# Pooled attention and two MLPs on one core: the second tile of the second MLP prepared earlier, and its accumulating matmuls moved by one place

## The chip, the cores and the metric

The kernel runs on one core of one Trainium2 chip. The metric is the device time of the program in microseconds (us), the median of several runs. Before the change three runs took 1678.56, 1679.4 and 1681.44 us, so the median is 1679.4 us.

## The reference

`q`, `k` and `v` have the shape (8, 8, 576, 64). Keys and values are averaged over groups of 8 positions, and attention runs over the 72 pooled positions. Its output is laid out as x, 4608 tokens by 512, and passes two MLPs, each 512 to 2048 to 512:

```python
h = x @ w_in                        # first MLP
g = where(h >= 1, h, where(h <= -1, 0, (h + 1) ** 2 / 4))
x = g @ w_out
h = x @ w_in2                       # second MLP
out = (h / (1 + exp(-h))) @ w_out2
```

Values are carried as pairs of float16 numbers (high and low part), so that each product takes three matmuls.

## The kernel before

**First MLP (A).** It works on 9 tiles of 512 tokens. A tile has 16 steps; a step is one block of 128 hidden values: 12 matmuls for h (`emit_h`, tile `hps`), the activation on ScalarE (ACT) and VectorE (DVE), a split into two float16 parts, and three steps later (`LAG`) 12 matmuls into the four accumulators `y0` to `y3` (`emit_yA`). After the last step of a tile `evac_yA` scales the four accumulators into `y32`, a room of the pool `big`, which has one buffer only, and stores them to DRAM (`ydram`).

**Second MLP (B).** It works on 18 tiles of 256 tokens. `tile_B` prepares a tile in six pieces: `load` reads `yin` from `ydram` into the room `big`; `look` takes the largest absolute value (DVE), spreads it over the partitions by a small matmul (`all_max`, tile `all`) and works out scales; `sums_` makes four sums of blocks on GpSimd (POOL) within `yin`; three `part` pieces split everything into the float16 pair `xh`, `xl` (pool `xs`, two buffers). `room` in the changed kernel is what gets that pair.

`group_B(t, q, ys)` then works on one half (q) of the hidden values with a seven-product scheme in place of eight: products 0 to 6 are 24 matmuls each (`hb`), in two banks of `ps_h` and two of `ps_a`. DVE adds them up to four blocks of h, ACT takes the activation, POOL forms four more combinations, ACT and DVE split seven operands (`g`). The seven accumulating products of a group (`py`, 12 matmuls each, in the order 0, 3, 4, 6, 5, 1, 2, into the banks `y0` to `y3`, two products to a bank) are handed on as a list `ys`, and are issued one by one within the next group by the calls `y(n)`. After the group of q = 0, when the last seven products of the tile before are in, `evac_yB` reads the four banks out with one ACT and seven DVE operations, and the result is stored.

**Order of the work.** The program text gives priorities; a planner orders each engine's instructions ahead of time by its own estimate of when each is ready, so that an instruction can stand ahead of others that come earlier in the text. At run time each engine takes its instructions strictly in that order. SyncE (SP) issues all transfers.

**Around the change.** In the last tile of A the list `pend` holds the six pieces of `tile_B(0)`, one per step from step m = 3. The first weights of B's second product (`wd`, `w4[0:4]`) are loaded during A, the other four after `wctx.close()`, into the room of A's weights. Line numbers: `load` L865, `look` L868 to L874 with its max L111 and its matmul L107, sums L681, splits L354 and L355, adds L910, accumulating products L973 to L975, `evac_yB` L985 to L998, `evac_yA` L846 to L849.

Of the kernel before, what the change touches and what calls it, by code (L numbers as in the profile page):

```python
# [9 lines left out]
F32 = mybir.dt.float32  # L10
F16 = mybir.dt.float16
I32 = mybir.dt.int32
AF = mybir.ActivationFunctionType
# [20 lines left out]
def tile_pooled_attention_two_mlps(  # L34
# [18 lines left out]
    nc = tc.nc  # L53
# [5 lines left out]
    N = 512  # L59
    NTILE = NT // N  # L60
# [632 lines left out]
    def comb_b(z, b11, b12, b21, b22):  # L693

        minus(z[1], b12, b11)
        minus(z[2], b22, z[1])
        minus(z[3], b22, b12)
        minus(z[0], b21, z[2])
# [140 lines left out]
    def evac_yA(t):  # L839
        r = XT.pop(t)  # L840
        cy = sm.tile([128, KD], F32, tag="cy", name="cy")
        ts(cy, e2, r["ge"], 2.0 ** -29, ALU.mult, ALU.mult)
        y = big.tile([128, KD, N], F32, tag="big", name="y32")
        for d, ps in enumerate(acc_t.pop(t)):
            if d % 2:
                ts(y[:, d], ps, cy[:, d:d + 1])  # L846
            else:
                nc.scalar.activation(out=y[:, d], in_=ps, func=AF.Copy, scale=cy[:, d:d + 1])
            nc.sync.dma_start(out=ydram[t][:, d], in_=y[:, d])  # L849


    TB = 256
# [4 lines left out]
    def tile_B(t):  # L857

        r = XB[t] = small(e=1, s=1, c1=1, ge=1, sg=1)
        held = {}  # L860

        def load():
            y = big.tile([128, 2, KD, TB], F32, tag="big", name="yin")
            held["y"], held["z"] = y[:, 0], y[:, 1].rearrange("p n (c f) -> p n c f", c=2)
            nc.sync.dma_start(out=held["y"], in_=ydram[t // 2][:, :, t % 2 * TB:(t % 2 + 1) * TB])  # L865
            held["b"] = held["y"].rearrange("p (h c) (n f) -> p h n c f", h=2, n=2)

        def look():  # L868
            m = sm.tile([128, 1], F32, tag="m1", name="m1")
            abs_max(m, held["y"])  # L870
            to_scale(r["e"], r["s"], m, FLOOR, 12)
            ts(r["c1"], e3, r["e"], 2.0 ** -24, ALU.mult, ALU.mult)
            ts(r["ge"], e3, r["e"], 2.0 ** -2, ALU.mult, ALU.mult)
            bits(r["sg"], r["ge"], -1.0, 254)  # L874

        def sums_():
            b = held["b"]
            comb_b([held["z"][:, n] for n in range(4)], b[:, 0, 0], b[:, 0, 1], b[:, 1, 0], b[:, 1, 1])
            r["x"] = [x.rearrange("p c n -> p (c n)")[:, 0:7 * 256].rearrange("p (n c f) -> p n c f", n=7, c=2)
                      for x in new_x()]  # L880

        def part(a, b, x):
            hi, lo = (y[:, a:b] if b > a + 1 else y[:, a] for y in r["x"])
            split(hi, lo, x(), r["s"])

        return [load, look, sums_, lambda: part(0, 2, lambda: held["b"][:, :, 0]),
                lambda: part(2, 3, lambda: held["b"][:, 1, 1]), lambda: part(3, 7, lambda: held["z"])]

    def group_B(t, q, ys):

        r = XB[t]
        xh, xl = r["x"]
        pool = (gp, gp2)[q]
        gt = {}

        def product(n, i):
            p, tag = ((ps_h, "h"), (ps_a, "a"))[n // 2 % 2]
            ps = p.tile([128, 4, 128], F32, tag=tag, name="hb")
            for j in range(4):
                w = w3[4 * q + j]  # L900
                for k_ in range(2):
                    three(ps[:, j], w[:, 0, i, k_], w[:, 1, i, k_], xh[:, i, k_], xl[:, i, k_],
                          j == 0 and k_ == 0, j == 3 and k_ == 1)
            return ps

        def new_c():
            return cp.tile([128, 4, 128], F32, tag="c", name="c")

        def add(out, x, y):
            nc.vector.tensor_tensor(out=out, in0=x, in1=y, op=ALU.add)  # L910

        def act(x):
            nc.scalar.activation(out=x, in_=x, func=AF.Silu, scale=r["c1"])  # L913

        def halves_of(i, x):
            to = gt[i] = pool.tile([128, 2, N], F16, tag="g", name="g16")
            split(to[:, 0], to[:, 1], x.rearrange("p j n -> p (j n)"), r["sg"])

        def y(n):
            for _ in range(n):  # L920
                if ys:
                    ys.pop(0)()

        c11, u, v, c22, z1, z2, z3, z4 = (new_c() for _ in range(8))
        nc.scalar.copy(out=u, in_=product(0, 0))
        add(c11, u, product(1, 1))
        act(c11)
        halves_of(0, c11)
        y(1)
        add(u, u, product(2, 5))  # L930
        y(1)
        add(v, u, product(3, 6))
        y(1)
        p5 = product(4, 4)
        add(c22, v, p5)
        act(c22)
        add(u, u, p5)
        halves_of(3, c22)
        y(1)
        c12 = u  # L940
        add(c12, u, product(5, 2))
        act(c12)
        plus(z1, c12, c22)
        minus(z3, c11, c12)
        minus(z2, z1, c11)
        y(1)
        c21 = v
        add(c21, v, product(6, 3))
        act(c21)
        halves_of(4, z1)  # L950
        halves_of(6, z3)
        y(1)
        halves_of(5, z2)
        minus(z4, c21, z2)
        halves_of(1, c21)
        halves_of(2, z4)
        y(1)
        if q == 0:
            r["acc"] = [ps_y.tile([128, 2, 256], F32, tag=f"y{k_}", name=f"y{k_}") for k_ in range(4)]

        def py(i):
            out = r["acc"][i // 2][:, i % 2]
            first = q == 0 and i == next(n for n in ORDER if n // 2 == i // 2)
            last = q == 1 and i == [n for n in ORDER if n // 2 == i // 2][-1]
            gh, gl = gt[i][:, 0], gt[i][:, 1]
            for j in range(4):
                f, w = slice(128 * j, 128 * j + 128), w4[4 * q + j]
                three_r(out, gh[:, f], gl[:, f], w[:, 0, i], w[:, 1, i], first and j == 0, last and j == 3)

        return [lambda i=i: py(i) for i in ORDER]  # L970
# [180 lines left out]
    for s in range(KF, LAST + LAG):  # L1151
        T, m = divmod(s, KF)
        if s < LAST:
            emit_h(s, chunk1, XT[T]["x"])
        z = s - 1
        if KF <= z < LAST:
            pre_A(z, XT[z // KF])
            min_A(z, XT[z // KF])
        if KF + 1 <= z <= LAST:
            late["gl"] = split_g(z - 1, XT[(z - 1) // KF])  # L1160
        if KF <= z < LAST:
            mid_A(z, XT[z // KF])
            post_A(z, XT[z // KF])
        for _ in range(2 if KF < s <= KF + XS else 1):
            if slots_left:
                next_slot()
        if not slots_left and b1 is None:
            att_ctx.close()
            b1 = bctx.enter_context(tc.tile_pool(name="b1", bufs=1, reuse_waits="tile"))
        want = todo_n * (s - KF + 1) // (SPREAD * KF // 4)  # L1170
        while todo and todo_n - len(todo) < want:
            paced(todo.pop(0), "gl")
        if b1 and not w3 and len(todo) <= left3:
            for i in range(PIECES):
                w3.append(b1.tile([128, 2, 7, 2, 128], F16, name=f"wc{i}"))
                nc.sync.dma_start(out=w3[i].rearrange("p a n c f -> p a n (c f)"), in_=d3[:, i])
        if w3 and not w4 and not todo:
            conv_ctx.close()
            b1 = bctx.enter_context(tc.tile_pool(name="b1w", bufs=1, reuse_waits="tile"))
            for i in range(4):  # L1180
                w4.append(b1.tile([128, 2, 7, 256], F16, name=f"wd{i}"))
                nc.sync.dma_start(out=w4[i], in_=d4[:, i])
        if T == NTILE - 1 and m == 3:
            pend.extend(tile_B(0))
        if pend:
            pend.pop(0)()
        z = s - LAG
        if z >= KF:
            emit_yA(z)
            if z % KF == KF - 1:  # L1190
                evac_yA(z // KF)

    wctx.close()
    b2 = bctx.enter_context(tc.tile_pool(name="b2", bufs=1, side="right", reuse_waits="tile"))
    for i in range(4, PIECES):
        w4.append(b2.tile([128, 2, 7, 256], F16, name=f"wd{i}"))
# [3 lines left out]
    ys = []  # L1200
    for t in range(NTB):
        for q in range(2):
            if t + 1 < NTB:
                if q == 0:
                    pend.extend(tile_B(t + 1))
                for _ in range(3):
                    pend.pop(0)()
            ys = group_B(t, q, ys)
            if q == 0 and t:
                evac_yB(t - 1)  # L1210
    for f in ys:
        f()
    evac_yB(NTB - 1)
# [31 lines left out]
```

## Time and profile before

| | |
|---|---|
| median of 3 runs | 1679.4 us |
| the profiled execution | 1683.29 us |
| its span, first to last instruction | 1681.4 us |
| granted TensorE clock, mean | 0.965 of full speed |
| TensorE matmuls (PE) busy | 1561.3 us, 93% |
| VectorE (DVE) busy | 1255.0 us, 75% |
| ScalarE (ACT) busy | 894.9 us, 53% |
| GpSimd (POOL) busy | 534.7 us, 32% |
| TensorE leaves A, enters B | at 972.38 us |

Busy time of PE counts a matmul from its issue to its modelled end, and neighbours overlap; a matmul row's duration (0.22 or 0.27 us) is therefore longer than its share of the engine, which is the distance to the next row's start. A bracket at the end of a row of the timeline gives the idle time of that engine ahead of it, and the instruction that ended it.

### The profile page before, as it was taken

How to read it: one execution, taken by the hardware profiler on the slowest of the kernel's cores; microseconds unless marked ns; L12 is line 12 of the kernel's file. 1: busy time of each engine (PE TensorE's matmuls, PEld its weight loads, DVE VectorE, ACT ScalarE, POOL GpSimd, SP SyncE). 2: the span in 40 equal slices, each digit the busy share in tenths (PEclk: the TensorE clock that was granted, in tenths of full speed). 3: DMA queues.
4: the chain of work that ended last, by engine and by line, in shares of the span. 5: the costliest groups of instructions: out<-in, count | busy, mean ns of one | idle time of the engine just before them, and what ended most of it. 6: DMA issues, size and time to landing. Idle time of an engine off the chain costs nothing.

```text
span 1681.4 us, 34695 instructions
## 1 busy us (share of the span) xinstructions
PE 1561.3 (93%) x14406; PEld 1078.8 (64%) x14406; DVE 1255.0 (75%) x2204; ACT 894.9 (53%) x1420; POOL 534.7 (32%) x479
## 2 busy tenths in 40 slices
PE   6894799898999999999999979999999999999998
PEld 6542344344444444444444459999999999999998
DVE  7798887978889787897656338777766777777765
ACT  3577354666747547576655435455444454444543
POOL 1322402332424303333422023443333343334322
PEclk7897899899999999999999989999999999999999
DMA  9435587655646576353454030000100001000000
GB/s 278 129 99 140 140 218 174 145 129 137 166 118 161 141 218 167 98 131 86 133 220 148 0 138 27 27 27 27 37 30 27 27 27 39 27 27 27 27 14 27
DMA packets 217037, 166.35 MB, mean 99 GB/s; under 512 B 153904, under 2 KB 176432, under 8 KB 216880
## 3 DMA queue, kind: packets, MB, share of 16 engines
q1 hardware_dynamic: 216880, 164.14, 35.1%
q8 instruction: 113, 1.85, 0.5%
q14 instruction: 44, 0.36, 0.1%
HBM read 102.76 MB, written 33.55 MB: 81 GB/s over the span
## 4 chain that ended last, share of the span: by engine, by line
PE 31%; DVE 26%; issue 15%; ACT 10%; DMA 8%; POOL 8%; SPq 1%; DVEq 0%; POOLq 0%; ACTq 0%
DMA yin<-y 4%; PE y L120 4%; PE y L122 4%; PE y L121 4%; POOL c L681 4%; DVE sum L420 4%; DVE g L355 4%; PE hps L122 4%; PE hps L121 4%; PE hps L120 4%; DVE g L791 3%; POOL c L684 2%; DVE xl L355 2%; DVE g L820 2%; ACT g L354 2%
## 5 line engine op out<-in xcount | busy, mean ns | idle before, releaser
L121 PE MATMUL hb<-xl,wc 128*128 128x128 f16 x2016 | 349.7, 219 | 0.0
L120 PE MATMUL hb<-xh,wc 128*128 128x128 f16 x2016 | 349.7, 219 | 0.0
L122 PE MATMUL hb<-xh,wc 128*128 128x128 f16 x2016 | 349.7, 219 | 0.0
L355 DVE SCALAR_TENSOR_TENSOR g<-c,tsg,g 128x512 f16<-128x512 f32 x252 | 226.6, 902 | 87.8 <-ACT g L354 87.8
L973 PE MATMUL y<-wd,g 128*128 128x256 f16 x1008 | 274.7, 273 | 14.4 <-DVE ob L986 13.0
L975 PE MATMUL y<-wd,g 128*128 128x256 f16 x1008 | 274.8, 273 | 1.0 <-DVE g L355 0.9
L974 PE MATMUL y<-wd,g 128*128 128x256 f16 x1008 | 274.7, 273 | 0.0
L913 ACT ACTIVATE c<-c,tc 128x512 f32<-128x512 f32 x144 | 103.0, 717 | 258.8 <-DVE c L910 258.8
L120 PE MATMUL y<-g,wb 128*128 128x512 f16 x544 | 207.7, 388 | 17.3 <-ACT wb L212 15.0
L120 PE MATMUL hps<-xh,wa 128*128 128x512 f16 x576 | 221.0, 384 | 1.3 <-ACT g L780 0.9
L354 ACT ACTIVATE g<-c,tsg 128x512 f16<-128x512 f32 x252 | 177.6, 718 | 83.7 <-POOL c L684 51.3
L121 PE MATMUL hps<-xl,wa 128*128 128x512 f16 x576 | 220.9, 383 | 0.3 <-DVE skv L95 0.3
L122 PE MATMUL hps<-xh,wa 128*128 128x512 f16 x576 | 220.6, 384 | 0.0
L910 DVE TENSOR_TENSOR c<-c,hb 128x512 f32<-128x512 f32 x252 | 167.7, 680 | 70.4 <-PE hb L122 70.1
L121 PE MATMUL y<-g,wb 128*128 128x512 f16 x544 | 211.2, 388 | 5.8 <-DVE g L820 5.8
L122 PE MATMUL y<-g,wb 128*128 128x512 f16 x544 | 210.5, 387 | 4.1 <-POOL wb L213 3.9
L121 PEld LDWEIGHTS <-wc 128*128 128x128 f16 x2016 | 197.7, 98 | 2.6
L120 PEld LDWEIGHTS <-wc 128*128 128x128 f16 x2016 | 197.7, 98 | 2.1
L122 PEld LDWEIGHTS <-wc 128*128 128x128 f16 x2016 | 197.7, 98 | 0.2
L791 DVE SCALAR_TENSOR_TENSOR g<-g,tbr,u 128x512 f32<-128x512 f32 x144 | 127.4, 886 | 59.2 <-ACT u L787 58.0
L681 POOL TENSOR_TENSOR c<-c 128x512 f32<-128x512 f32 x108 | 163.8, 1530 | 2.8
L787 ACT ACTIVATE u<-u,trsg 128x512 f32<-128x512 f32 x144 | 103.3, 719 | 103.8 <-DVE u L93 103.8
(179 smaller groups left out, 2719.7 us busy)
## 6 DMA issues: line engine op xcount, KB each, us to landing
raw<-in_moe_w_out_dram SPq DMA_DIRECT2D x24, 1024.0 KB
raw<-in_moe_w_in_dram SPq DMA_DIRECT2D x18, 1024.0 KB
raw<-in_k_dram SPq DMA_DIRECT2D x32, 288.0 KB
raw<-in_v_dram SPq DMA_DIRECT2D x32, 288.0 KB
y<-y SPq DMA_DIRECT2D x36, 256.0 KB
yin<-y SPq DMA_DIRECT2D x18, 512.0 KB
out_dram<-ob SPq DMA_DIRECT2D x36, 256.0 KB
qt<-in_q_dram SPq DMA_DIRECT2D x32, 256.0 KB
```

The lines of the kernel that those rows point to most:

```text
L120: nc.tensor.matmul(out=acc, lhsT=wh, rhs=xh, start=start, stop=False)
L121: nc.tensor.matmul(out=acc, lhsT=wh, rhs=xl, start=False, stop=False)
L122: nc.tensor.matmul(out=acc, lhsT=wl, rhs=xh, start=False, stop=stop)
L354: a = nc.scalar.activation(out=hi, in_=x, func=AF.Copy, scale=s)
L355: return a, nc.vector.scalar_tensor_tensor(out=lo, in0=x, scalar=s, in1=hi, op0=ALU.mult, op1=ALU.subtract)
L681: nc.gpsimd.tensor_tensor(out=out, in0=a, in1=b, op=ALU.subtract)
L787: nc.scalar.activation(out=u_t[s], in_=u_t[s], func=AF.Square, scale=r["rsg"])
L791: return nc.vector.scalar_tensor_tensor(out=g32_t[s], in0=g32_t[s], scalar=r["br"], in1=u_t.pop(s), op0=ALU.subtract, op1=ALU.max)
L910: nc.vector.tensor_tensor(out=out, in0=x, in1=y, op=ALU.add)
L973: nc.tensor.matmul(out=acc, lhsT=xh, rhs=wh, start=start, stop=False)
L974: nc.tensor.matmul(out=acc, lhsT=xh, rhs=wl, start=False, stop=False)
L975: nc.tensor.matmul(out=acc, lhsT=xl, rhs=wh, start=False, stop=stop)
```

## The change

Four edits. Of `tile_B(1)` the first three pieces (load, look, sums) follow those of tile 0 in the last tile of A; its parts come ahead of the second group. To make room in `big`, the last `y32` goes to four tiles of the pool `up`. The pair `xh`, `xl` is asked for at the first part, not at the sums. In a group of q = 1 the first call `y(1)` becomes `y(0)` and the last `y(2)`, so that six of the seven places take one product later. For later tiles the load is issued at the end of the tile two before, and look and sums ahead of the next group, which is the same place in the text as before.

```diff
@@ evac_yA
-        y = big.tile([128, KD, N], F32, tag="big", name="y32")
+        if t < NTILE - 1:
+            y = big.tile([128, KD, N], F32, tag="big", name="y32")
+            ys = [y[:, d] for d in range(KD)]
+        else:
+            ys = [up.tile([128, N], F32, tag="gu"[d % 2], name="y32") for d in range(KD)]
         for d, ps in enumerate(acc_t.pop(t)):
             if d % 2:
-                ts(y[:, d], ps, cy[:, d:d + 1])
+                ts(ys[d], ps, cy[:, d:d + 1])
             else:
-                nc.scalar.activation(out=y[:, d], in_=ps, func=AF.Copy, scale=cy[:, d:d + 1])
-            nc.sync.dma_start(out=ydram[t][:, d], in_=y[:, d])
+                nc.scalar.activation(out=ys[d], in_=ps, func=AF.Copy, scale=cy[:, d:d + 1])
+            nc.sync.dma_start(out=ydram[t][:, d], in_=ys[d])
@@ tile_B
+
+        def room():
             r["x"] = [x.rearrange("p c n -> p (c n)")[:, 0:7 * 256].rearrange("p (n c f) -> p n c f", n=7, c=2)
                       for x in new_x()]
         def part(a, b, x):
+            if a == 0:
+                room()
@@ group_B
         add(c11, u, product(1, 1))
         act(c11)
         halves_of(0, c11)
-        y(1)
+        y(1 - q)
...
         halves_of(2, z4)
-        y(1)
+        y(1 + q)
@@ the last tile of A
         if T == NTILE - 1 and m == 3:
             pend.extend(tile_B(0))
+            rest = tile_B(1)
+            pend.extend(rest[:3])
+            rest = rest[3:]
@@ B
+    pend = rest
...
     for t in range(NTB):
         for q in range(2):
-            if t + 1 < NTB:
-                if q == 0:
-                    pend.extend(tile_B(t + 1))
-                for _ in range(3):
-                    pend.pop(0)()
+            for _ in range(min(len(pend), 3 if q else 2 if t else 0)):
+                pend.pop(0)()
             ys = group_B(t, q, ys)
             if q == 0 and t:
                 evac_yB(t - 1)
+        if t + 2 < NTB:
+            pend = tile_B(t + 2)
+            pend.pop(0)()
```

## Rows read from the trace of the kernel before

**Rows 1.** The page: busy us of an engine, share of the span, instructions.
```profile
PE 1561.3 (93%) x14406; PEld 1078.8 (64%) x14406; DVE 1255.0 (75%) x2204; ACT 894.9 (53%) x1420; POOL 534.7 (32%) x479
```

**Rows 2.** Windows: stretch, length, busy us (instructions) by engine, granted clock, DMA share, GB/s.
```profile
940.00:960.00 20.00, 20.00 (x94) 9.11 (x93) 7.62 (x12) 7.88 (x12) 0.00 (x0) 1.00 0.00 1
...
972.38:1016.50 44.12, 31.57 (x425) 28.61 (x424) 22.87 (x38) 16.60 (x24) 12.89 (x13) 0.88 0.38 132
...
978.65:989.83 11.18, 0.98 (x9) 0.64 (x8) 1.22 (x1) 0.00 (x0) 1.05 (x2) 0.69 0.77 305
...
989.83:993.20 3.37, 3.37 (x29) 3.31 (x30) 2.16 (x10) 1.64 (x3) 1.76 (x3) 0.50 0.02 5
...
1023.85:1063.36 39.51, 37.87 (x514) 35.71 (x512) 30.64 (x52) 19.84 (x30) 14.74 (x12) 1.00 0.08 29
...
1561.80:1599.30 37.50, 36.99 (x501) 34.96 (x499) 27.34 (x47) 18.22 (x28) 14.39 (x12) 1.00 0.08 30
...
1599.30:1636.40 37.10, 37.10 (x508) 35.20 (x506) 25.49 (x39) 16.50 (x26) 11.56 (x8) 1.00 0.05 16
```

**Rows 3.** Waits of PE, 960 to 1016.6 us: us in total, times, longest.
```profile
PE all L107 <- DVE m L111: 10.2, 1, 10.2
```

**Rows 4.** Waits of PE, 1020 us to the end.
```profile
PE y L973 <- DVE ob L986: 13.0, 17, 1.5
```

**Rows 5.** Timeline of PE at the start of B: start, us, operation, count, [idle before].
```profile
979.36 0.27 PE L975 MATMUL y<-wd,g 128*128 128x256 f16 x1
...
989.83 0.80 PE L107 MATMUL all<-ident,m 128*128 128x128 f32 x2 [10.20 <-DVE m L111]
...
1016.28 0.39 PE L107 MATMUL all<-ident,m 128*128 128x128 f32 x2
1016.50 0.22 PE L120 MATMUL hb<-xh,wc 128*128 128x128 f16 x1
```

**Rows 6.** Timeline of DVE at the start of B.
```profile
977.56 0.75 DVE L355 SCALAR_TENSOR_TENSOR g<-c,tsg,g 128x512 f16<-128x512 f32 x1 [1.54 <-ACT g L354]
988.56 1.22 DVE L111 TENSOR_REDUCE m<-yin 128x1 f32<-128x1024 f32 x1 [10.25 <-DMA yin<-y]
```

**Rows 7.** Timeline of SP's issues around the end of A.
```profile
972.00 1.82 SPq L849 DMA_DIRECT2D y<-y  x4
973.91 2.19 SPq L1197 DMA_DIRECT2D wd<-d  x4
978.64 0.55 SPq L865 DMA_DIRECT2D yin<-y  x1
```

**Rows 8.** Timeline of POOL at the start of B.
```profile
988.78 2.89 POOL L681 TENSOR_TENSOR yin<-yin 128x256 f32<-128x256 f32 x4 [79.45 <-DMA yin<-y]
```

**Rows 9.** The tile yin: duration ns min/median/max, first and last start.
```profile
L354 ACT ACTIVATE xh<-yin,ts x54: 492/722/1137, 912.5 to 1597.0; 128x512 f16<-128x512 f32 x18, 128x256 f16<-128x256 f32 x18, 128x1024 f16<-128x1024 f32 x18
```

**Rows 10.** Timeline of ACT at the end of A.
```profile
971.28 0.69 ACT L848 ACTIVATE y<-y,cy 128x512 f32<-128x512 f32 x1 [5.52 <-PE y L122]
```

**Rows 11.** Timeline of PE in two groups of q = 1, tiles 10 and 8.
```profile
1382.73 0.22 PE L120 MATMUL hb<-xh,wc 128*128 128x128 f16 x1
...
1385.41 0.27 PE L973 MATMUL y<-wd,g 128*128 128x256 f16 x1
...
1388.77 0.27 PE L973 MATMUL y<-wd,g 128*128 128x256 f16 x1 [0.49 <-DVE ob L986]
...
1305.32 0.22 PE L120 MATMUL hb<-xh,wc 128*128 128x128 f16 x1
...
1312.80 0.27 PE L973 MATMUL y<-wd,g 128*128 128x256 f16 x1 [1.49 <-DVE ob L986]
```

**Rows 12.** Timeline of DVE in the first of these groups.
```profile
1383.88 0.48 DVE L986 SCALAR_TENSOR_TENSOR ob<-y,cyb,ub 128x256 f32<-128x256 f32 x1
...
1388.25 0.86 DVE L986 SCALAR_TENSOR_TENSOR ob<-y,cyb,ub 128x256 f32<-128x256 f32 x2
1389.03 0.67 DVE L910 TENSOR_TENSOR c<-c,hb 128x512 f32<-128x512 f32 x1
```

## The prediction, made before the changed kernel ran

> **What bounds the kernel now.** I read the page first: TensorE (PE) is busy 93% of the span [rows 1], so the question is where its 7% go and which of that the change touches. The windows place it. In A the engine is busy in every microsecond (20.00 of 20.00 at clock 1.00), while DVE works 7.62 and POOL nothing [rows 2]: A is bound by PE, and small work put beside it has cover. At the step from A to B PE has 31.57 busy of 44.12 us. In the steady part of B, 15 tiles take from 1023.85 to 1599.30, 575.45 us (the first and the last window of them are shown), 38.36 us each, against 37.10 us for the tile behind them, in which PE is busy without a gap [rows 2]. That tile has no scale matmul `all`; one costs 0.22 us (1016.28 to 1016.50 [rows 5]), so a tile without waits is 37.32 us, and 15 of them lose 575.45 - 15 x 37.32 = 15.65 us. The list of waits names the causes: one wait of 10.2 us for the max of tile 1 [rows 3], and 17 waits of 13.0 us together for `evac_yB` to free a bank [rows 4]. (13.0 is idle alone; the distance between starts adds some 0.17 us each, which gives the 15.65.)
>
> **Part 1: tile 1 prepared within A.** The order of events in the old transition: the last `y32` is stored from `big` and the four `wd` are issued from 973.91; only then, at 978.64, does SP issue `yin` of tile 1, since `big` was taken [rows 7]. DVE, strictly in order, stands before the max of that tile until 988.56 [rows 6], some 9.9 us after the issue; PE stands before its `all` from the end of the last matmul (979.36 + 0.11) to 989.83, 10.36 us [rows 5]. The granted clock then is 0.50 for the 3.37 us after the stall, the lower level of 1.2 GHz [rows 2]; at the upper level these take half, 1.7 us less. The stall and its slow stretch are worth 10.36 + 1.7 = 12.05 us.
>
> What is moved, and its cover. Load, four sums and max go before the end of A, when `big` is free (tile 0's parts are done there, and no `y32` follows in it). POOL stood idle for 79.45 us before these sums, whose 2.89 us [rows 8] therefore push nothing. The max is 1.22 us on DVE [rows 6], with seven tiny operations after it, in A's 38% loaded DVE [rows 2]. The `all` costs PE 0.22 us there as here. On SP the load passes the four stores and the `wd`, 0.55 us of issue ahead of them [rows 7]. So I take 0 for the move; if the cover failed, DVE would stand before a late load in A, at the worst 9.9 us as here; below zero I see nothing, as PE has no gap in A to give back. The parts of tile 1 (three splits on each engine, at most 1.14 us each on ACT [rows 9]) become possible when A's last `hps` matmul has read its pair; ACT has 5.52 us free before it reads the accumulators [rows 10]. The four small rooms for the last y cost nothing: the same four copies, in rooms that the last steps of A have left; the other bound is one copy's delay, 0.69 us [rows 10].
>
> What is late next at the transition: 14 products at 1.34 us (48 matmuls from 1382.73 to 1385.41 are 2.68) and 7 accumulating ones of 1.31 us (37.10 = 14 x (1.34 + 1.31)) make 27.93 us, with the two `all` 28.4, of the 44.12. After 12.05 some 3.7 us of other waits remain, ACT, POOL and DVE coming late with the first g. Some of it may go, since POOL no longer has tile 1's sums in B; I leave all 3.7 in, keeping 0 and 3.7 as bounds of a further gain. Part 1: **12.05 us**.
>
> For tile 2 the trace has a hint on the queue. What was issued at 978.64 behind the four `wd` landed only 9.9 us later [rows 6, 7]. The Trainium skill, "DMA: Bandwidth & Descriptors", section "Queues, rings and completion order", says that each DMA engine consumes descriptors in ring order: by that rule a later load cannot pass the `wd`, and if `yin` of tile 2 is issued behind them it is as late as tile 1's was; the trace agrees. Priced as rival A.
>
> **Part 2: the accumulating products one place later.** In a group of q = 1 the second accumulating product (the first into its bank) waits for DVE's last readings of the old tile: PE at 1388.77, DVE's last pair beginning at 1388.25 [rows 11, 12]. From the group's start at 1382.73 this is 6.04 us. Before it PE has three products and one accumulating one; after the change four and one, 4 x 1.34 + 1.31 = 6.67 us, so the bank is free 0.63 us before it is asked for. The first accumulating product (bank `y0`) also moves 1.34 us back. Where the wait is longest, tile 8, the release is 1312.80 - 1305.32 = 7.48 us after the start [rows 11], and 0.81 us of wait remain. Five tiles have waits of this kind (1.26 to 1.49 us), ten have 0.46 to 0.70 (the rows show one of each). For the five I take a remainder of 2.2 us in all, between 0 and 5 x 0.81 = 4.1. The gain is 15.65 - 2.2 = **13.45 us**.
>
> Behind the moved product stand the rest of PE's queue, and products that wait for DVE's adds. Three products now run in a row; the trace shows two. The third needs a `ps_a` bank, emptied by an add of the group before. I take 0; the other end is one add late, 0.67 us [rows 12], in each of 17 groups, 11.4 us; below zero, the adds can begin 1.31 us earlier. No matmul is added: the two at the group's end are the one taken from its head. In the last tile the seven products that follow PE's last group keep their number, so the tail stays.
>
> The windows show clock 1.00 in all these tiles, short waits included [rows 2]. The Trainium skill, "TensorE: Matmul & The Clock Gate", section "A second HAM failure mode: psum-queue depth-cycling", says that frequent short idles between groups make the clock fall and rise again. By that rule, 15 waits removed would give back 15 slow stretches of 1.7 us as well, 25 us more; the trace disagrees, as 1.00 leaves nothing to give back, and I count none.
>
> **Sum.** 12.05 + 13.45 = 25.5 us. The profiled execution took 1683.29 us, 1.9 around a span of 1681.4; it would become 1657.8. It stands 3.9 us above the median of 1679.4; against the median the forecast is **1653.9 us**.
>
> **The rivals.**
>
> *A, the stall moves to tile 2.* Its load follows tile 1's parts. If the planner sets those after A's end, the load goes out behind the `wd`, and a max set early in DVE's queue stops DVE as before. For: exactly this happened with tile 1 [rows 6, 7]. Against: ACT and DVE have room for the parts before 971.28, so that the load can pass the `wd`, and tile 2's max is needed a whole tile later in the text. DVE would stand from about 980 to 988.6; PE could run some four products (5.4 us) on free banks, and lose 4 to 10 us. With 7 lost: 1661.
>
> *B, the evacuation's wait moves along.* If the planner puts the now earlier adds of products 1 and 2 in front of DVE's last readings, these end 2 x 0.67 = 1.34 us later; the 0.63 us of room turns into 0.71 us of wait, in 15 tiles 10.7, and with the 2.2 part 2 gives 2.8 in place of 13.45: 1664.5. For: DVE shows no idle time from 1383.88 to the add that ends at 1389.70 [rows 12]. Against: the readings come earlier in the text.
>
> *C, tile 1 is not ahead.* The planner keeps its load behind A's end after all, for instance since it sees DVE or `big` as taken; then part 2 alone comes: 1666. Against: the load's room is free a dozen steps earlier.
>
> *D, neither.* A and B at their worst: within 3 us of 1679.4.
>
> *E, slower.* One mechanism: three products in a row, while product 5 reuses the bank that the add of product 1 frees. That add ends at 1389.70 [rows 12]; product 5 would start at 1382.73 + 5 x 1.34 + 3 x 1.31 = 1393.4. It decides from 3.7 us of delay of that add; to eat 25.5 us in 17 groups takes 1.5 us more, 5.2 in all. With DVE 6 us late, 2.3 x 17 = 39 us are lost: 1679.4 - 25.5 + 39 = 1693. For: DVE is the fullest helper, 75%. Against: it has idle stretches in every half tile.
>
> **Chances.** Forecast 0.60; A 0.14; B 0.10; C 0.06; D 0.05; E 0.05. What a measurement of this kernel can tell from no change is about 0.2%, 3.4 us. Faster is the forecast with A, B and C, 0.90; D is the same, 0.05; E is slower, 0.05. The range: at best both losses vanish with the other waits, 12.05 + 3.7 + 15.65 = 31.4, so 1648, less 1.5 for the scatter of the runs (1678.56 to 1681.44): 1646.5. Upward it takes in A, B and C and part 1 alone (1679.4 - 12.05 = 1667.4): 1668.
>
> **What would show it.** Right: PE's wait for the max at the start of B is gone and the clock stays 1.00 there; `yin` of tile 1 is issued in A with PE busy 20.00 of 20 around it; the waits of accumulating products for `evac_yB` fall from 13.0 to about 2 us; 15 tiles take about 562 us. A long DMA wait of DVE just after A's end shows A; the old list of waits shows B; `yin` after 973.91 shows C; waits of product matmuls for adds show E. A gain below 15 us would make the prediction wrong in one of its two parts.

## The result

The changed kernel takes 1650.16 us (median of 4 runs, 1647.97 to 1653.04), the kernel before 1680.35 us in 4 runs (1678.56 to 1681.44): a ratio of 0.9822, 95% interval 0.9801 to 0.9844, or 30.2 us less. The forecast was 1653.9 us, 25.5 less.

### The profile page after: what moved, and what is told of

Read it like the earlier page. It is cut to its first block, busy times and chain, and to the rows that moved or that the text cites. A ratio compares the mean times of both kernels' runs of the same rounds, so it can differ in the third digit from the quotient of the medians.

```text
span 1649.7 us, 34708 instructions
## 1 busy us (share of the span) xinstructions
PE 1558.8 (94%) x14406; PEld 1081.0 (66%) x14406; DVE 1261.8 (76%) x2204; ACT 895.6 (54%) x1420; POOL 533.6 (32%) x479
## 4 chain that ended last, share of the span: by engine, by line
PE 44%; DVE 24%; issue 9%; ACT 9%; DMA 7%; POOL 7%; SPq 0%; DVEq 0%; POOLq 0%; ACTq 0%
DVE sum L420 5%; POOL c L681 4%; PE y L120 4%; PE y L122 3%; PE y L121 3%; PE hps L121 3%; PE hps L120 3%; PE y L981 3%; PE y L983 3%; PE y L982 3%; PE hps L122 3%; PE hb L121 3%; PE hb L120 3%; PE hb L122 3%; DVE g L791 3%
## 5 line engine op out<-in xcount | busy, mean ns | idle before, releaser
L791 DVE SCALAR_TENSOR_TENSOR g<-g,tbr,u 128x512 f32<-128x512 f32 x144 | 123.4, 858 | 56.8 <-ACT u L787 55.6
```

Source lines behind the costliest of these rows:

```text
L791: return nc.vector.scalar_tensor_tensor(out=g32_t[s], in0=g32_t[s], scalar=r["br"], in1=u_t.pop(s), op0=ALU.subtract, op1=ALU.max)
```

## The profile after, beside the one before

Two stages answer for most of it. The first is the transition, from the last accumulating matmul of A to the first product of B's tile 1; the second is all that lies behind. The windows of the changed kernel (columns as in [rows 2]), A's last steps first:

```profile
940.00:966.43 26.43, 26.43 (x124) 11.96 (x122) 11.51 (x17) 11.28 (x17) 0.00 (x0) 1.00 0.06 20
966.43:969.53 3.10, 3.10 (x23) 1.68 (x22) 1.89 (x2) 0.86 (x2) 2.66 (x4) 1.00 0.02 5
969.53:997.18 27.65, 27.65 (x415) 26.70 (x414) 19.18 (x27) 15.95 (x23) 9.57 (x8) 1.00 0.49 173
997.18:1649.70 652.52, 644.22 (x8684) 610.06 (x8681) 478.59 (x797) 314.84 (x477) 241.19 (x198) 1.00 0.08 28
```

A ends at 969.53; nine of B's matmuls (0.50 us) were put ahead of its last twelve, so B's first tile holds TensorE for 27.65 + 0.50 = 28.15 us, where it took 44.12 [rows 2]. The engine is busy in all of it, and the granted clock is 1.00, the upper level, where the kernel before had a stretch at 0.50. That is 15.97 us; 0.22 of it is no gain, since the scale matmul `all` of tile 1 now stands in A. Behind it are 652.5 us where there were 1681.4 - 1016.50 = 664.9: 12.4 us less. The remaining 3.35 us lie ahead, in A and the attention (A's end 972.38 against 969.03). Together 31.7, the difference of the two spans.

SP's issues show the moved load. The first `yin` below is tile 1's, within A; the second is tile 2's, also ahead of the stores and of the four `wd`, where before even tile 1's came behind them [rows 7]:

```profile
913.15 0.54 SPq L869 DMA_DIRECT2D yin<-y  x1
...
963.10 0.52 SPq L869 DMA_DIRECT2D yin<-y  x1
969.21 1.80 SPq L853 DMA_DIRECT2D y<-y  x4
971.09 2.23 SPq L1209 DMA_DIRECT2D wd<-d  x4
```

DVE's two maxima, of tile 1 and tile 2, wait 1.12 and 1.57 us for their transfers where tile 1's waited 10.25 [rows 6]:

```profile
916.76 1.22 DVE L111 TENSOR_REDUCE m<-yin 128x1 f32<-128x1024 f32 x1 [1.12 <-DMA yin<-y]
...
966.68 1.22 DVE L111 TENSOR_REDUCE m<-yin 128x1 f32<-128x1024 f32 x1 [1.57 <-DMA yin<-y]
```

POOL's sums of both tiles lie in A too, where before those of tile 1 ran in B [rows 8]. The third row is POOL's first work in B, a combination of the first group:

```profile
916.87 3.34 POOL L681 TENSOR_TENSOR yin<-yin 128x256 f32<-128x256 f32 x4 [11.06 <-DMA yin<-y]
966.79 2.90 POOL L681 TENSOR_TENSOR yin<-yin 128x256 f32<-128x256 f32 x4 [46.57 <-DMA yin<-y]
978.84 1.27 POOL L684 TENSOR_TENSOR c<-c 128x512 f32<-128x512 f32 x1 [9.15 <-ACT c L921]
```

TensorE's waits from 960 us to the end are one line, where [rows 3] and [rows 4] had 10.2 and 13.0 us:

```profile
PE y L981 <- DVE ob L994: 2.7, 3, 1.4
```

And the steady tiles: tile 1 starts at 997.18, tile 16 at 1560.74, so 15 tiles take 563.6 us (forecast about 562; before, between the same two points, 575.7). The three waits left are in the tiles 7, 8 and 9: 0.54, 0.77 and 1.42 us. The rows of tile 8 and of tile 9, each with the start of its group of q = 1:

```profile
1278.18 0.22 PE L120 MATMUL hb<-xh,wc 128*128 128x128 f16 x1
...
1285.79 0.27 PE L981 MATMUL y<-wd,g 128*128 128x256 f16 x1 [0.77 <-DVE ob L994]
...
1316.44 0.22 PE L120 MATMUL hb<-xh,wc 128*128 128x128 f16 x1
...
1324.70 0.27 PE L981 MATMUL y<-wd,g 128*128 128x256 f16 x1 [1.42 <-DVE ob L994]
```

In tile 8 the bank comes free 7.61 us after the group's start (before, 7.48 [rows 11]). In tile 9 it comes 8.26 us after it, where before it was 6.06. What sets that moment stands further up in DVE's queue: the max of the tile two ahead, which waits for that tile's load. Before, in tiles 8 and 9:

```profile
1299.34 1.22 DVE L111 TENSOR_REDUCE m<-yin 128x1 f32<-128x1024 f32 x1 [3.23 <-DMA yin<-y]
...
1337.34 1.22 DVE L111 TENSOR_REDUCE m<-yin 128x1 f32<-128x1024 f32 x1 [1.80 <-DMA yin<-y]
...
1350.80 0.27 PE L973 MATMUL y<-wd,g 128*128 128x256 f16 x1 [0.51 <-DVE ob L986]
```

And in tile 9 of the changed kernel, SP's issue of the load and DVE's max:

```profile
1305.72 0.53 SPq L869 DMA_DIRECT2D yin<-y  x1
...
1311.23 1.22 DVE L111 TENSOR_REDUCE m<-yin 128x1 f32<-128x1024 f32 x1 [3.73 <-DMA yin<-y]
```

TensorE's waiting matmul starts 13.46 us after the max in tile 8 before (1312.80 [rows 11]), 13.46 in tile 9 before, 13.47 in tile 9 now. In all twelve kernels the readings of that bank end 13.4 us after the max begins in 175 of 180 tiles; the other five are first tiles. So in the steady tiles the waits for the evacuation follow the landing of a load: the max began 5.5 us after the issue in tile 9 now, 3.6 us in tile 9 before. No run moved these loads.

## The experiments

The table gives time and ratio to the kernel before (measured anew with e1 to e4, with e5 to e8, and with e9 and e10: 1680.48, 1679.16 and 1679.04 us). From the profile it gives A's end (without the 0.50 us of products put ahead of it), the transition, what lies behind, and TensorE's waits for the evacuation, all in us. The transitions of 28.4 us (e1, e8) hold two `all`, those of 28.15 one.

| kernel | us | ratio, 95% | A's end | transition | behind | waits for the evacuation |
|---|---|---|---|---|---|---|
| before | 1680.35 | | 972.38 | 44.12 | 664.9 | 13.0 |
| changed | 1650.16 | 0.9801 to 0.9844 | 969.03 | 28.15 | 652.5 | 2.7 |
| e1_rooms | 1661.4 | 0.9876 to 0.9914 | 963.85 | 28.38 | 665.2 | 13.8 |
| e2_shift | 1662.15 | 0.9881 to 0.9912 | 964.75 | 44.86 | 652.8 | 3.0 |
| e3_early | 1663.91 | 0.9885 to 0.9916 | 969.93 | 28.16 | 664.3 | 13.0 |
| e4_wd_after | 1670.42 | 0.9928 to 0.9957 | 965.14 | 36.16 | 663.8 | 12.1 |
| e5_two_places | 1653.62 | 0.9818 to 0.9866 | 968.22 | 28.16 | 654.9 | 1.7 |
| e6_tile2_behind | 1650.5 | 0.9787 to 0.9843 | 961.05 | 28.15 | 650.4 | 1.1 |
| e7_before_again | 1680.86 | 0.9989 to 1.0022 | 970.81 | 44.53 | 665.6 | 13.5 |
| e8_rooms_shift | 1650.13 | 0.9803 to 0.9854 | 966.82 | 28.37 | 653.2 | 3.5 |
| e9_order | 1646.59 | 0.9781 to 0.9825 | 964.62 | 28.15 | 649.5 | 0 |
| e10_after_order | 1649.48 | 0.9799 to 0.9852 | 968.13 | 28.15 | 650.7 | 1.6 |

### e1: the four rooms alone

```diff
-        y = big.tile([128, KD, N], F32, tag="big", name="y32")
+        if t < NTILE - 1:
...
+            ys = [up.tile([128, N], F32, tag="gu"[d % 2], name="y32") for d in range(KD)]
```

> The kernel before with one edit: the last y32 of A leaves through four rooms of the pool up, so that big is free when A ends; the text of tile_B and the accumulating products stay as before. Theory (the stall came from the load of tile 1 being late, because its only room was taken): the planner can now issue that load in A, TensorE's wait for the max at the start of B falls from 10.2 us to under 1, the clock stays 1.00 there, and the time falls by 12 us, 13 to 16 if the other waits of the transition go as well; the evacuation's 17 waits stay at about 13 us. Rival A (the stall moves to tile 2, whose load now goes out behind the wd): a wait of 4 to 10 us appears within 30 us of A's end and the time falls by 2 to 8 us only. Rival C (what counts is the place in the text): no change.

The transition fell by 15.7 us, to no wait at all; the evacuation's waits stayed. The time fell by 19 us, more than the stages behind A give (see e7). With the text of `tile_B` unmoved, SP issued tile 1's load in A all the same, and tile 2's behind the `wd`. First the windows, then SP's issues:

```profile
963.85:992.23 28.38, 28.38 (x426) 27.41 (x425) 23.13 (x38) 17.51 (x26) 12.63 (x11) 1.00 0.54 187
```

```profile
908.26 0.55 SPq L869 DMA_DIRECT2D yin<-y  x1
963.53 1.79 SPq L853 DMA_DIRECT2D y<-y  x4
965.42 2.26 SPq L1201 DMA_DIRECT2D wd<-d  x4
970.42 0.53 SPq L869 DMA_DIRECT2D yin<-y  x1
```

So the room alone was enough to let the load out early. This experiment's rival C (the place in the text) falls. Rival A had its condition, tile 2 behind the `wd`, and its price was zero, by a narrow margin. POOL, which stood for the same load, could start at 981.30, 10.9 us after the issue, so it landed as late as tile 1's did before, or later. DVE had other work until then, and its max followed without idle time:

```profile
981.26 1.21 DVE L111 TENSOR_REDUCE m<-yin 128x1 f32<-128x1024 f32 x1
...
981.30 3.82 POOL L681 TENSOR_TENSOR yin<-yin 128x256 f32<-128x256 f32 x4 [0.50 <-DMA yin<-y]
```

### e2 and e3: each part alone

```diff
 e2, on the kernel before            e3, on the changed kernel
-        y(1)                       -        y(1 - q)
+        y(1 - q)                   +        y(1)
...
-        y(1)                       -        y(1 + q)
+        y(1 + q)                   +        y(1)
```

> The kernel before with one edit: in a group of q = 1 the first y(1) becomes y(0), the last y(2). Theory (the accumulating products came 0.5 to 1.5 us too early for the evacuation, and one product more in front of them covers it): the waits of accumulating products for the evacuation fall from 13.0 to 2 to 4 us, the stall of 10.2 us at the start of B stays, time 12 to 13.5 us less. Rival B (the evacuation's last readings move back as adds come earlier): 10 to 13 us of waits remain, time 0 to 4 us less.

> The changed kernel with y(1) and y(1) put back: only tile 1's earlier preparation and its rooms remain. Theory (the two parts are independent and add up): the transition takes 28.2 us as in the changed kernel, the evacuation's waits are back at 13 us; time 16 us under the kernel before (1664), 12 to 14 above the changed kernel. Rival (the moved accumulating products also fill the first groups of B, so that the last 3.7 us of the transition were theirs): 12 us under the kernel before, with 3 to 4 us of waits of TensorE between A's end and the second tile.

e2: the waits for the evacuation fall to 3.0 us, the stall stays, and what lies behind the transition is 652.8, 12.1 us less. Its whole time fell by 18.3, more than the second MLP gives; its A ended 7.6 us earlier, see e7. TensorE's waits in e2, from A's end on:

```profile
PE all L107 <- DVE m L111: 10.8, 1, 10.8
PE y L973 <- DVE ob L986: 3.0, 4, 1.3
PE y L973 <- ACT g L354: 1.4, 3, 0.7
PE y L975 <- DVE g L355: 0.9, 2, 0.6
```

e3: the transition is 28.16 us as in the changed kernel, with TensorE busy in all of it, and the waits are back at 13.0. In the profiles the two parts add up: from A's end to the end of the span 709.0 before, 697.7 with e2, 692.5 with e3; 11.4 and 16.5 are 27.9, and the changed kernel has 28.3 less. In whole times they do not: 18.3 and 16.6 are 34.9 against 30.2. That the last 3.7 us of the transition belong to the moved products (the rival of e3) is refuted: they are gone without them.

### e4: the queue, without the room

```diff
-        nc.sync.dma_start(out=w4[i], in_=d4[:, i])
...
+            if t == q == 0:
+                with tc.issue_after(late["yin"].ins):
+                    for i in range(4, PIECES):
+                        nc.sync.dma_start(out=w4[i], in_=d4[:, i])
```

> The kernel before with one edit: the four last wd are issued after the load of tile 1 instead of before it; the room big is still taken until A's last y is stored. Theory (most of the 10.2 us is the transfer standing behind 3.6 MB of wd): the load lands 5 to 6 us after its issue or sooner instead of 9.9, TensorE's wait for the max falls to 1 to 4 us, time 7 to 10 us less. Rival (the late room alone is the cause, the queue is not): the wait stays at 8 us or more, time within 2 us of before. If the wd now come too late, waits for DMA appear at the accumulating products of the second group.

The room still comes only after A's end, but the load no longer stands behind the `wd`. It went out at 969.53, 4.4 us after A's end (before, 6.3, with the `wd` issued in between), and DVE had its max at 973.13, 3.6 us later and not 9.9 [rows 6, 7]. TensorE's wait for it is 2.0 us in place of 10.2, of which some 6.3 us come from the shorter way of the load and 1.9 from its earlier issue. The time falls by 10 us, the transition by 8.0. Tile 2's load, behind the `wd` here, was what DVE stood for next:

```profile
973.13 1.22 DVE L111 TENSOR_REDUCE m<-yin 128x1 f32<-128x1024 f32 x1 [2.06 <-DMA yin<-y]
...
986.72 1.22 DVE L111 TENSOR_REDUCE m<-yin 128x1 f32<-128x1024 f32 x1 [3.74 <-DMA yin<-y]
```

```profile
PE y L975 <- DVE g L355: 2.4, 2, 2.2
PE all L107 <- DVE m L111: 2.0, 1, 2.0
PE hb L120 <- DVE c L910: 0.9, 1, 0.9
```

Here rival A is seen at work: DVE idles 3.74 us and TensorE stands 2.2 us behind it for one g. Most of the stall's length was the queue's; that the load was in that queue at all was the room's.

### e5: one more place

```diff
         y(1 - q)
         add(u, u, product(2, 5))
-        y(1)
+        y(1 - q)
...
-        y(1 + q)
+        y(1 + 2 * q)
```

> The changed kernel with the accumulating products of a group of q = 1 one more place later: the first two calls are y(0), the last y(3). Theory (what is left of the waits, 2.7 us at three places, is the same release coming 7 to 8 us after the group's start): they vanish, the part from A's end to the end of the span falls from 680.7 us to 677 to 678, nothing new waits. Rival (without two accumulating products at its head TensorE outruns DVE's adds): waits of product matmuls for adds appear, over 0.2 us in each of 17 groups, and that part grows by 3 us or more.

The theory was wrong: what lies behind the transition grew by 2.4 us. The rival was nearer, but not right either: it asked for 3 us or more and for waits for DVE's adds in each of 17 groups. The old wait didn't go entirely, and a new one came at four places, at products that wait for ACT's copy of the first product out of its bank:

```profile
PE hb L120 <- ACT c L933: 2.6, 4, 1.0
PE y L981 <- DVE ob L994: 1.7, 5, 0.3
```

### e6: tile 2's load held back behind the wd

```diff
-            pend.pop(0)()
+            with tc.issue_after(late["wd"].ins) if t == 0 else nullcontext():
+                pend.pop(0)()
```

> The changed kernel with one edit: the load of tile 2 must be issued behind the four wd. It prices rival A of the prediction. Theory (DVE takes its queue in order and stands before the max of tile 2 until the load lands, as it did for tile 1): the load lands 8 to 11 us after its issue, DVE idles 3 us or more before that max, TensorE loses 1 to 6 us in waits for DVE before the second tile, and the transition takes 29 to 34 us in place of 28.2. Rival (the load is late but nothing needs tile 2 yet): DVE's wait stays under 1 us or costs TensorE nothing, 28.2 us.

The theory was wrong, the rival right: 28.15 us. The load went out at 965.44, behind the `wd`, and it landed 12.8 us later, when POOL's sums of tile 2 could start (978.25). But in DVE's queue the max stood behind adds and splits, and DVE came to it 0.2 us after that:

```profile
965.44 0.61 SPq L869 DMA_DIRECT2D yin<-y  x1
```

```profile
977.86 0.67 DVE L918 TENSOR_TENSOR c<-c,hb 128x512 f32<-128x512 f32 x1
978.46 1.21 DVE L111 TENSOR_REDUCE m<-yin 128x1 f32<-128x1024 f32 x1
```

In these runs a late load cost something only where an instruction that needs it stood early in a queue, as tile 1's max did before, and tile 2's in e4. Why the planner set that max early in e4 and late in e1 and e6 was not tried, and with margins of 0.2 us and less the zero cost is partly luck.

### e7: the kernel before once more

> The kernel before once more, unchanged, as a control: how much does the part ahead of the second MLP vary from one execution to the next? Theory (it varies by some us with the arrival of transfers, the second MLP doesn't): A's end lies between 963 and 972 us, the part behind it is within 1 us of the 709.0 of the first profile. Rival (the edits move A's end): A's end is at 972 again, within 1 us.

Unchanged, it took 1674.51 to 1684.13 us in 10 runs. Its second MLP repeated: 44.53 and 665.6 us, 710.1 together against 709.0, just outside the 1 us of the theory. A's end came at 970.81, within the theory's bounds and 1.6 us from the first profile, too near to it to choose. Over all profiles A ends between 961.05 and 972.38 us, and e6 alone, with runs from 1641.36 to 1654.14, shows a wide scatter in one kernel. In e2 scatter does not explain it: by its interval its time fell by 14.8 to 20.0 us, and the second MLP gives 11.4. Yet up to A's end every engine runs the same instructions in the same order in e2 as in the kernel before, so the new order of the work is not the cause; what is stays open. For the second MLP I therefore trust the stages of the profiles more than the totals.

### e8: rooms and places, without the early text

> The kernel before with two edits: the four rooms for the last y32, and the accumulating products one place later; the text of tile_B stays where it was. Theory (the rooms alone free the load of tile 1, its place in the text adds nothing, and both gains add up): from A's end to the end of the span 709.0 - 15.5 - 11.4 = 682 us, 1 us from the changed kernel's 680.7; time as the changed kernel's. Rival (the earlier text is needed for the parts of tile 1 and the load of tile 2): 3 to 10 us longer than the changed kernel.

1650.13 us, and 681.6 us from A's end on, against 680.7: the changed kernel without the moved text is as fast, within the 1.1 us by which e7 and the first profile differ there. The other edits, in `tile_B` and in the loop, do nothing that these runs can tell.

### e9 and e10: another order in place of another place

```diff
-    ORDER = [0, 3, 4, 6, 5, 1, 2]
+    ORDER = [0, 6, 3, 4, 5, 1, 2]
```

e9 is this edit on the kernel of e3, e10 on the changed kernel.

> The kernel of the second experiment but one (tile 1 early, accumulating products at their old places) with their order changed from 0, 3, 4, 6, 5, 1, 2 to 0, 6, 3, 4, 5, 1, 2. The evacuation reads product 6 (alone in bank y3) fifth and products 2 and 3 (bank y1) sixth and seventh of its eight operations. Theory (the wait is for bank y1, asked for by the second accumulating product; a product of another bank in its place moves that request 2.65 us back): the 13.0 us of waits fall under 2, from A's end to the end of the span 692.5 becomes 679 to 681, as with the moved places. Rival (the wait is for DVE as a whole, whichever bank is asked for): 10 us or more of waits remain. Second rival (product 6's operand isn't ready so early): waits for ACT's or DVE's g appear.

> The changed kernel with the order 0, 6, 3, 4, 5, 1, 2. Theory (the bank y1 is then asked for 4 us later than in the kernel before, past the latest release of 7.7 us after the group's start): no wait of accumulating products for the evacuation is left, from A's end to the end of the span 677 to 678.5 in place of 680.7; time 1647 to 1650, within the scatter of the part ahead. Rival (the last 3 us are not waits but the planner's order around them): 680 to 681.

e9 has no wait of TensorE left behind A's end, in transition and steady part: 28.15 + 649.5 = 677.7 us, 3 less than the changed kernel. Its windows, and TensorE's list of waits from 965 us on is empty:

```profile
965.12:992.77 27.65, 27.65 (x415) 26.70 (x414) 19.16 (x27) 15.95 (x23) 9.53 (x8) 1.00 0.49 173
992.77:1642.30 649.53, 643.91 (x8684) 609.95 (x8681) 474.51 (x797) 313.10 (x477) 241.23 (x198) 1.00 0.08 29
```

So the wait was for one bank, y1, and not for DVE as a whole: asking for y3 in its place was enough, though DVE's readings of y1 end as late as in e3 (up to 7.3 us after the group's start in e9, 7.5 in e3). With 1646.59 us e9 is the fastest kernel of the study, against 1680 and 1650 (its A ended early as well, so of the 3.6 us to the changed kernel the profile vouches for 3). e10, with both cures, is 678.9 us, between its theory and its rival. Bank y1 is waited for no more; 1.6 us of waits at two places remain, of the first accumulating product, for bank y0, and its total is within the scatter of both.

## Why the prediction was right

**Place and mechanism.** Both parts of the sum were found where it put them: the wait for tile 1's max gone and the clock at 1.00, the waits for the evacuation from 13.0 to 2.7 us (forecast about 2), load and sums of tile 1 in A without a gap of TensorE. e2 and e3 show them apart. Of the edits of part 1 the rooms alone were needed (e1, e8), a question that the prediction did not ask.

**Part 1 was mis-sized**, 12.05 forecast, 15.97 measured, 15.75 without the moved `all`; e1, with both `all` in place, has 15.7 too. The failing term is "after 12.05 some 3.7 us of other waits remain", kept in the sum whole, with a bound of 3.7 more: all of it went. The trace of the kernel before shows what it was. One wait of 0.25 us lies ahead of the stall: TensorE had four products to do and then stood for a g (978.37). In the changed kernel ten products run ahead of the first accumulating one. Four waits, 1.97 us together, lie behind the stall, and the first is at the end of this chain:

```profile
999.00 2.55 POOL L681 TENSOR_TENSOR yin<-yin 128x256 f32<-128x256 f32 x3 [7.33 <-DMA yin<-y]
1001.51 1.26 POOL L684 TENSOR_TENSOR c<-c 128x512 f32<-128x512 f32 x1
...
1002.80 0.72 ACT L354 ACTIVATE g<-c,tsg 128x512 f16<-128x512 f32 x1 [3.49 <-POOL c L684]
...
1003.58 0.28 PE L973 MATMUL y<-wd,g 128*128 128x256 f16 x1 [0.68 <-ACT g L354]
```

POOL stood for the load of tile 2, not of tile 1, and made three of its sums before the combination that ACT needed. The prediction looked at POOL, but at tile 1's sums. DVE's late adds had their share: ACT stood 2.89 us for one at 996.61. No run takes these causes apart: in e1, e3 and the changed kernel all are gone together, while in e4, where POOL's combinations come first, TensorE stands 2.2 us for DVE.

**Part 2**: 13.45 forecast, 12.4 measured (12.1 alone). The remainder was taken as 2.2 us; it is 2.7 of idle time, and the rest of the difference is within the 1.1 us by which this stage repeats. In tile 8 it is 0.77 us, and 0.81 was foreseen. The step that did not hold is that the release keeps its distance from the group's start: the prediction took the old trace's distances, at most 7.48 us, and in tile 9 it was 8.26, for 1.42 of the 2.7 us. It goes with the landing of a load, which in tile 9 came 1.9 us later after its issue than in the trace before. The prediction did not name that load.

**The rest.** 15.97 + 12.4 are 28.3 us of the 31.7 between the profiles; the other 3.35 lie ahead of the change, in a part that scatters by more than that. No step of the prediction accounts for them.

**The rivals.** A: in the changed kernel tile 2's load passed the `wd`; its condition came in e1 and e6, without its price; only e4 paid it. B: not seen, in e2 and the changed kernel the waits fell. C: the load of tile 1 went out in A, at 913.15, so it did not come. D: neither part failed. E: the nearest to it is e5, where one place more did make products wait, 2.6 us in all.

## What to carry to other kernels

Where an engine waits long for a load, ask first what the load waited for before it was issued: here one room of a one-buffer pool, and freeing it was worth the whole first half. Of a wait for a bank, ask which bank, when it is read in the release, and what the reading engine stood for before that; another order of the requests can do as much as more work in front. And when a stall is taken out, follow the short waits around it back to their own releasers; here they went with it.

## What was not expected

The part ahead of the second MLP ends anywhere from 961 to 972 us over twelve profiles, and ten runs of one unchanged kernel spread over 9.6 us, while the second MLP repeats within 1.1 us in two profiles of that kernel. A load issued behind four `wd` (tile 2's, in e1 and e6) cost nothing at all, where the same position cost tile 1's 10 us before: it landed as late, but its reader came later in DVE's queue. And the short waits for a bank in the second MLP, which look like DVE's, have a load behind them: the bank came free a fixed 13.4 us after the max that stood for it. In tiles 16 and 17, which have no such max, the readings of that bank ended 4.6 us after the group's start in the kernel before and in the changed one, and TensorE did not wait.
